# Hash attention and a gated feed-forward on one core: a new order of the first microseconds, one PSUM bank apart, and another issuer for the last pieces

## The chip, the core and the metric

The kernel runs on one core of a Trainium2 chip. The core has a matrix engine (TensorE, PE in the profile, with PEld for its weight loads), VectorE (DVE), ScalarE (ACT), GpSimd (POOL) and the sync engine (SP); SP, ACT and POOL can issue DMAs. The metric is device time in microseconds, the median of several runs.

## The reference, cut to what matters

```python
B, H, S, D = 4, 8, 768, 64            # attention; then 3072 tokens, 512 -> 2048 -> 512
q_bits = einsum(q, proj) > 0           # 6 bits; k_bits likewise
mask   = bucket(q_bits)[:, None] == bucket(k_bits)[None, :]
scores = where(mask, q @ k.T / 8, -1e9)
attn   = softmax(scores) @ v
x      = attn with heads side by side  # (3072, 512)
h      = x @ w_in
out    = (h * erf(softplus(h))) @ w_out
```

All inputs are float32.

## The kernel before, in words

**Attention.** The 32 heads are worked in 16 pairs; the heads of a pair sit on the partitions 0 to 63 and 64 to 127. For each pair TensorE hashes q and k with `proj`, ScalarE takes the signs, and signs and bucket weights become bfloat16 rows `qb` and `kb` whose product is zero where the buckets agree and hugely negative where they do not. A score tile `st` (128 keys, two heads of 384 queries) is the sum of two products, one of these bits and one of the float32 q and k. A pair has four groups of three such tiles: `score(n, c)` with n counting groups over all pairs and c from 0 to 2. ScalarE's `exponential` writes each tile to `e_all`, VectorE adds up the keys (`sum_keys`), and TensorE's `weigh` multiplies with v into `av` (L631). ScalarE's `leave` copies `av` out of PSUM (L690); the division by the sums follows later.

**Two ways for the bits.** Pair 0's bits are taken directly. `hash_bits` (L373) makes both halves of the rows with 64 output columns for q and 64 for k, one half of the 768 positions at a time; `take_bits` is ScalarE's sign (L386), two VectorE multiplies by the bucket weights (`spread_bits`, L397) and a VectorE copy (`double_bits`, L407), into the tile `both[0]`. All later pairs go another way: `bits_of` (L812) packs q and k of both halves into four groups of 32 columns, `sign_of` and `weigh_bits` work on the packed tile `sg`, `leave_bits` (L841) sends it to DRAM and `place_bits` (L850) brings it back into the right rows of `both[i % 2]`. The unused rows of `both` have to be zero: GpSimd clears `both[1]` at the start (L433), and `clean` (L859) clears `both[0]` after pair 0.

**PSUM.** Tiles of the tag `big` are two banks each, three of them: hashes and scores take them in turn, in the order in which they are allocated. `bank(...)` is one bank under one tag, and each call allocates it anew. `av` has one bank of the pool `psum`. In the feed-forward the pool `ps_f` holds seven banks, `M1` to `M7`.

**Order.** The start is written out by hand: loads, then `WARM` matmuls on a tile of ones (L780), then hashes and bits of pair 0. From there a planner, `arrange`, orders operations for each engine from estimated costs, ranks and due times; TensorE's own order is fixed by a list (`order`, `chain`), in which the first scores are followed by pair 1's bits, then `weigh`, and so on. VectorE and ScalarE also turn the weights into float32 between these operations, while GpSimd fetches the weights' pieces.

**Feed-forward.** Both matrix products use Strassen-like sums in blocks: seven products `P1` to `P7` (L1183) for the first, seven accumulations `M1` to `M7` (L1323) for the second, over six tiles of 512 tokens with four steps each. `combine` (L1354) adds the seven sums into output pieces and issues their DMA (L1362); `M3` is emptied last, in two halves k = 7 and k = 8. After that a flag decides on a general path, which these inputs do not need.

Of the kernel before, what the change touches and what calls it, by code (L numbers as in the profile page):

```python
# [54 lines left out]
F32 = mybir.dt.float32  # L55
# [8 lines left out]
P = 128  # L64
# [129 lines left out]
def kernel(  # L194
# [34 lines left out]
    small = ctx.enter_context(tc.tile_pool(name="small", bufs=3))  # L229
    QR = 32  # L230
    QB = QR // 2
    WARM = 5
    proj_sb = const.tile([P, 2 * QR], F32, name="proj_sb")
    weight = const.tile([P, 2], F32, name="weight")
    proj_q = const.tile([P, QR], F32, name="proj_q")
# [9 lines left out]
    blocks = []  # L245
    stats = const.tile([P, 2, NPAIR, 2], F32, name="stats")
    nc.vector.memset(ones, 1.0)
    nc.vector.memset(w_sum[:, 0, 0, 0:HS], 1.0)
    warm = w_sum[:, 0, 0, 0:HS]
    proj_in = const.tile([P, 2 * NBIT], F32, name="proj_in")  # L250
    nc.gpsimd.dma_start(out=proj_in, in_=proj2)
    nc.vector.memset(proj_sb, 0.0)
# [46 lines left out]
    def bank(name):  # L299
        return misc.tile([P, 512], F32, name=name, tag="bank")  # L300
# [108 lines left out]
    def take_bits(d, tile_of, halves=(0, 1)):  # L409
        cols = slice(halves[0] * HS, (halves[-1] + 1) * HS)  # L410
        sign_bits(d, tile_of, cols)
        for ab in (1, 0):
            spread_bits(d, cols, ab)
        double_bits(d, cols)

    def attention():
        NS = NPAIR * 4
        with (
# [4 lines left out]
            tc.tile_pool(name="rawp", bufs=2) as rawp,  # L423
            tc.tile_pool(name="cvt", bufs=1) as cvt,
            tc.tile_pool(name="psum", bufs=1, space=PSUM) as psum,
        ):

            def big(name):
# [1 line left out]

            sg = bitp.tile([P, HS], BF16, name="sg")
            both = [bitp.tile([P, 2, S], BF16, name=f"both{n}") for n in range(2)]
            nc.gpsimd.memset(both[1], 0.0)  # L433
            junk = ep.tile([P, HS], BF16, name="junk")
            NE = 3 * GC
            e_all = ep.tile([P, NE, 2, HS + 1], F32, name="e_all")
# [184 lines left out]
            def weigh(n):  # L621
                half, g = n // 2 % 2, n % 2
                d = pairs[n // 4]
                if g == 0:
                    d["av"] = psum.tile([P, 512], F32, name="av", tag="av")
                w = HS + 1 - half
                for c in range(GC):
                    e = block(n, c)
                    for ab in range(2):
                        rows = slice(ab * D, ab * D + D)  # L630
                        nc.tensor.matmul(  # L631
                            out=d["av"][rows, 0:w],
                            lhsT=d["v"][:, g * GC + c, rows],
                            rhs=e[:, ab, 0:w],
                            start=(g == 0 and c == 0),
                            stop=(g == 1 and c == GC - 1),
                        )
# [138 lines left out]
                pairs[i] = fetch(i, load)  # L776

            pairs[0] = fetch(0, load, quick=True)
            for n in range(WARM):
                nc.tensor.matmul(  # L780
                    out=bank("warm")[:, 0 : 2 * P],
                    lhsT=warm[:, 0:P],
                    rhs=warm[:, P:HS],
                    start=True,
                    stop=True,
                )
            for half in range(2):
                hash_bits(pairs[0], big, (half,))
                take_bits(pairs[0], lambda what: both[0][:, "qk".index(what[0]), :], (half,))

            NH = NPAIR * 2
            ops = []
# [5 lines left out]
            def pe(fn, args, cost, after=()):  # L798
                if chain:
                    after += (chain[-1],)  # L800
                op(fn, args, "PE", cost, (0, len(chain)), after, late=0.25)
                chain.append((fn.__name__,) + args)

            def bits_of(i):


                d = pairs[i]
                d["bits"] = big("bits")
                for n, what in enumerate("qk"):
                    for half in range(2):  # L810
                        row = (2 * n + half) * QR
                        nc.tensor.matmul(  # L812
                            out=d["bits"][row : row + QR, 0, 0:HS],
                            lhsT=proj_q,
                            rhs=d[what][:, half * HS : (half + 1) * HS],
                            start=True,
                            stop=True,
                        )
# [35 lines left out]
                        in_=bd[:, ab, 0 : NBIT + 1, :].rearrange("n r c -> r n c"),  # L854
                    )

            def clean():

                nc.gpsimd.memset(both[0], 0.0)  # L859

            chain = []
            order = [("score", 0)]
            for h in range(NH):
                order += [("score", n) for n in (2 * h + 1, 2 * h + 2) if n < NS]
                if h == 0:
                    order.insert(3, ("bits", 1))
                if h % 2 and (h + 3) // 2 < NPAIR:
                    order.append(("bits", (h + 3) // 2))
                if h >= 1:
                    order.append(("divisor", h - 1))  # L870
                order += [("weigh", 2 * h), ("weigh", 2 * h + 1)]
            slots = []
            for what, n in order:
                if what == "score":
                    i = n // 4
                    after = (("place_bits", i),)
                    if n == 0:
                        for c in range(2):
                            pe(plain, (n, c), 0.66)
                    for c in range(GC):  # L880
                        free = (slots[-3],) if len(slots) >= 3 else ()
                        pe(score, (n, c), 0.82 if n or c == 2 else 0.17, after + free)
                        slots.append(("exponential", n, c))
                elif what == "bits":
                    pe(bits_of, (n,), 0.92, (("start_pair", n), slots[-3]))
                    slots.append(("sign_of", n))
                elif what == "divisor":
                    pe(divisor, (n,), 0.42, (("sum_keys", n, last_sum(n)), ("keep_divisor", n - 1)))
                else:
                    h = n // 2  # L890
                    after = (("exponential", n, GC - 1),)
                    if n % 2 == 0:
                        after += (("leave", h - 1), ("leave_plain", (h - 1) // 2))
                    pe(weigh, (n,), 2.02, after)
# [42 lines left out]
            for i in range(NPAIR):  # L937
                n = 4 * i
                if i:
                    op(  # L940
                        start_pair,
                        (i,),
                        "SP",
                        3.6,
                        (0, n - 6),
                        (("weigh", n - 9), ("bits_of", i - 1))
                        + tuple(("measure", i - 3, m, half) for m in range(2) for half in range(2)),
                        late=3.5,
                    )
                    op(sign_of, (i,), "ACT", 0.6, (0, n - 6, 9), (("bits_of", i), ("leave_bits", i - 1)))  # L950
                    op(weigh_bits, (i,), "DVE", 0.33, (0, n - 6, 1), (("sign_of", i),))
                    op(leave_bits, (i,), "POOL", 0.7, (0, n - 6, 2), (("weigh_bits", i),), late=2.6)
                    op(
                        place_bits,
                        (i,),
                        "POOL",
                        1.2,
                        (0, n - 6, 3),
                        (("leave_bits", i), ("score", n - 5, 2)) + (("clean",),) * (i == 2),
                        late=2.6,  # L960
                    )
                for m in range(2):
                    for half in range(2):
                        op(
# [21 lines left out]
                )  # L986
                op(normalise, (i,), "DVE", 0.95, (0, n + 8, 4), (("widen", i), ("leave", 2 * i + 1)))
                op(send, (i,), "SP", 0.35, (0, n, 4), (("normalise", i),), late=2.2)
            op(clean, (), "POOL", 1.4, (0, 0), (("score", 3, 2),), late=0.3)
            for n in range(len(pieces)):  # L990
                op(
                    fetch_weights,
# [144 lines left out]
    def feed_forward(check, late):  # L1137
        again = late is None
        with (
# [3 lines left out]
            tc.tile_pool(name="work", bufs=1) as work,  # L1143
            tc.tile_pool(name="outp", bufs=1) as outp,
            tc.tile_pool(name="ps_f", bufs=1, space=PSUM) as ps_f,
        ):
            NTILE = NT // T
            NP = NTILE * NC4
# [6 lines left out]
            def product(p, name, where, first, last):  # L1155
# [19 lines left out]
                if first:  # L1175
                    if where == "X":
                        d[where] = bank("X")[:, :].rearrange("p (u t) -> p u t", u=2)
                    else:
                        d[where] = ps_f.tile([P, 2, TH], F32, name=where, tag=where)
                for u in range(2):  # L1180
                    f = (2 * c + u) * P
                    for kc in range(2):
# [123 lines left out]
            def project(p, name, k):  # L1306
# [11 lines left out]
                    M7=lambda: (d["h", 1][:, 0, :, :], w_block(c, 0, 1)),  # L1318
                )[name]()
                if c == 0 and k == 0:  # L1320
                    banks[name] = ps_f.tile([P, 2, TH], F32, name=name, tag=name)
                sub, u = divmod(k, 2)
                nc.tensor.matmul(  # L1323
                    out=banks[name][:, sub, :],
# [9 lines left out]
            def combine(t, k):  # L1334
# [24 lines left out]
                )  # L1359
                if where:  # L1360
                    r0 = t * T + where[0] * TH + subs.start * P
                    nc.sync.dma_start(  # L1362
                        out=out[
                            r0 : r0 + (subs.stop - subs.start) * P,
                            where[1] * TH : (where[1] + 1) * TH,
                        ].rearrange("(s p) d -> p s d", p=P),
                        in_=outs[into][:, subs, :],
                    )
# [395 lines left out]
```

## Time and profile before

| | |
|---|---|
| median of 10 runs | 919.16 us (918.52 to 920.0) |
| the profiled execution | 918.66 us, its span 916.8 us |
| PE, DVE, ACT, POOL busy | 99%, 89%, 84%, 5% |
| first hash on PE | 7.67 us |
| first complete score on PE | 12.30 us |
| pair 1's bits in place | 26.60 us |
| last av issued, first feed-forward product | up to 323.7, 324.23 us |
| last output DMA issued | 911.70 us |

A row of the profile's timeline gives start and duration in microseconds, engine, line of the kernel, operation, `out<-in`, shape and count, and in brackets how long the engine was idle before and which operation ended that. A row of the waits gives the waiting engine and line, then who released it, with the total, the number of times and the longest wait. The chain is the sequence of work that ended last, followed back from the last instruction.

### The profile page before, as it was taken

The numbers are of one execution on the slowest core, as the hardware profiler recorded it, in microseconds if no ns is written. First come the engines' busy times: TensorE is split into PE (matmuls) and PEld (weight loads), VectorE is DVE, ScalarE is ACT, GpSimd is POOL, SyncE is SP. The second block draws the span as 40 slices with busy tenths as digits, with TensorE's granted clock in tenths as the row PEclk, the third lists the DMA queues.
The fourth block names the chain that finished last, engine by engine and source line by source line (L and its number), as shares of the span: only waits on it lengthen the run. The fifth ranks groups of instructions, "written<-read, shape, count | busy, mean of one in ns | idle before, by whom it ended". The sixth has DMA issues, their size and how long they took to land.

```text
span 916.8 us, 13120 instructions
## 1 busy us (share of the span) xinstructions
PE 905.3 (99%) x5006; PEld 660.1 (72%) x5006; DVE 819.5 (89%) x1020; ACT 767.9 (84%) x1002; POOL 46.5 (5%) x83
## 2 busy tenths in 40 slices
PE   9999999999999999999999999999999999999997
PEld 4444444444444478888888888888888888888885
DVE  4899999999899979899999799988899889988995
ACT  5888887788887849999998998899989997899892
POOL 1211111111111000000000000000000000000000
PEclk9999999999999999999999999999999999999999
DMA  8455577655673131102022112211221121011201
GB/s 206 117 156 160 158 182 195 186 144 159 164 196 123 59 122 64 46 1 104 12 71 79 36 46 69 81 35 46 70 81 35 35 75 41 35 35 46 69 35 49
DMA packets 62966, 83.05 MB, mean 91 GB/s; under 512 B 34174, under 2 KB 47342, under 8 KB 62896
## 3 DMA queue, kind: packets, MB, share of 16 engines
q1 hardware_dynamic: 56672, 64.08, 24.3%
q0 software_dynamic: 6064, 17.86, 6.3%
q8 instruction: 41, 0.67, 0.3%
q14 instruction: 29, 0.24, 0.1%
q10 hardware_dynamic: 160, 0.20, 0.1%
HBM read 64.71 MB, written 17.40 MB: 90 GB/s over the span
## 4 chain that ended last, share of the span: by engine, by line
PE 95%; DVE 2%; DMA 1%; SPq 1%; ACT 0%; issue 0%; POOL 0%; DVEq 0%; ACTq 0%; POOLq 0%
PE M L1323 31%; PE X L1183 28%; PE st L550 16%; PE av L631 14%; PE M L1183 3%; PE z_ps L666 1%; PE bits L812 1%; DMA q<-in_qkT_dram 1%; SPq L358 1%; DVE e L1237 0%; DVE h L1265 0%; SPq L363 0%; DMA bd<-sg 0%; DMA both<-bd 0%; DVE S L1280 0%
## 5 line engine op out<-in xcount | busy, mean ns | idle before, releaser
L1250 DVE SCALAR_TENSOR_TENSOR e<-w,e 128x1024 f32<-128x1024 f32 x144 | 173.4, 1221 | 5.8 <-ACT w L1246 3.0
L568 ACT ACTIVATE e_all<-st 128x768 f32<-128x768 f32 x192 | 151.1, 812 | 14.0 <-PE st L550 12.6
L1246 ACT ACTIVATE w<-w,cq 128x1024 f32<-128x1024 f32 x144 | 160.6, 1143 | 1.9
L550 PE MATMUL st<-q,k 64*128 64x384 f32 x768 | 155.7, 484 | 0.0
L1323 PE MATMUL M<-w_out_sb,h 128*128 128x256 f32 x576 | 140.3, 380 | 0.4 <-DVE h L1265 0.4
L631 PE MATMUL av<-e_all,v 128*64 128x385 f32 (+1 forms) x768 | 131.2, 490 | 0.0
L1183 PE MATMUL X<-x,w_in_sb 128*128 128x256 f32 x512 | 121.2, 380 | 0.0
L1323 PEld LDWEIGHTS M<-w_out_sb,h 128*128 128x128 f32 x576 | 109.4, 190 | 15.7 <-DVE h L1265 1.1
L1183 PEld LDWEIGHTS X<-x,w_in_sb 128*128 128x128 f32 x512 | 97.2, 190 | 13.7 <-ACT h L1201 0.6
L631 PEld LDWEIGHTS av<-e_all,v 128*64 128x64 f32 x768 | 52.3, 136 | 67.5 <-issue 66.6
L550 PEld LDWEIGHTS st<-q,k 64*128 64x128 f32 x768 | 68.7, 189 | 35.4 <-issue 34.5
L1323 PE MATMUL M<-wt,S 128*128 128x256 f32 x384 | 93.5, 380 | 0.4 <-DVE S L1280 0.4
L1183 PE MATMUL X<-x_sum,w_sum 128*128 128x256 f32 x344 | 81.7, 381 | 1.8 <-ACT h L1201 1.8
L1323 PEld LDWEIGHTS M<-wt,S 128*128 128x128 f32 x384 | 73.0, 190 | 10.6 <-DVE S L1280 0.8
L1183 PEld LDWEIGHTS X<-x_sum,w_sum 128*128 128x128 f32 x344 | 65.1, 190 | 11.9 <-ACT h L1201 3.3
L1201 ACT COPY h<-X 128x512 f32<-128x512 f32 x85 | 49.0, 576 | 22.3 <-PE X L1183 21.4
L1227 DVE SCALAR_TENSOR_TENSOR w<-w,e 128x1024 f32<-128x1024 f32 x48 | 58.5, 1221 | 9.7 <-ACT w L1222 9.6
L550 PE MATMUL st<-both 64*128 64x384 bf16 x384 | 63.2, 324 | 0.4 <-DMA both<-bd 0.2
L1265 DVE TENSOR_TENSOR h<-h,e 128x1024 f32<-128x1024 f32 x48 | 58.0, 1221 | 5.8 <-ACT e L1261 5.5
L1241 ACT ACTIVATE w<-e 128x1024 f32<-128x1024 f32 x48 | 50.4, 1050 | 13.3 <-DVE e L1237 13.0
L1237 DVE TENSOR_TENSOR e<-e,w 128x1024 f32<-128x1024 f32 x48 | 57.5, 1218 | 2.7 <-ACT e L1233 2.6
L1205 DVE TENSOR_TENSOR h<-X,h 128x512 f32<-128x512 f32 x65 | 44.8, 690 | 16.3 <-PE X L1183 15.4
(133 smaller groups left out, 1378.0 us busy)
## 6 DMA issues: line engine op xcount, KB each, us to landing
wt<-wt SPq DMA_DIRECT2D x24, 768.0 KB, 4.1
raw<-in_w_out_dram POOLq DMA_DIRECT2D x16, 512.0 KB, 4.6
raw<-in_w_in_dram POOLq DMA_DIRECT2D x14, 512.0 KB, 4.3
v<-in_v_dram SPq DMA_DIRECT2D x32, 192.0 KB, 4.6
xs<-x SPq DMA_DIRECT2D x16, 384.0 KB, 2.7
q<-in_qkT_dram SPq DMA_DIRECT2D x30, 192.0 KB, 4.1
k<-in_qkT_dram SPq DMA_DIRECT2D x30, 192.0 KB, 4.3
r<-rd SPq DMA_DIRECT2D x30, 192.0 KB, 3.4
```

The costliest lines, as they stand in the source:

```text
L550: nc.tensor.matmul(out=st[:, ab, 0:HS], lhsT=d["k" + src][rows, keys], rhs=d["q" + src][rows, cols], start=(part == 0), stop=(part == 1),)
L568: nc.scalar.activation(out=e[:, :, 0:HS], in_=st[:, :, 0:HS], func=AF.Exp, scale=scale)
L631: nc.tensor.matmul(out=d["av"][rows, 0:w], lhsT=d["v"][:, g * GC + c, rows], rhs=e[:, ab, 0:w], start=(g == 0 and c == 0), stop=(g == 1 an ...
L1183: nc.tensor.matmul(out=d[where][:, u, :], lhsT=a[:, kc, f : f + P], rhs=b[:, kc, :], start=(first and u == 0 and kc == 0), stop=(last and ...
L1201: nc.scalar.copy(out=quarter(p, q), in_=st[p][where])
L1227: nc.vector.scalar_tensor_tensor(out=w, in0=w, scalar=-1.0, in1=st[p]["e", v], op0=ALU.add, op1=ALU.subtract)
L1237: nc.vector.tensor_tensor(out=s, in0=s, in1=st[p].pop(("w", v)), op=ALU.subtract)
L1241: nc.scalar.activation(out=z, in_=st[p]["s", v], func=AF.Square)
L1246: nc.scalar.activation(out=q, in_=z, func=AF.Square, bias=cq[:, j : j + 1])
L1250: nc.vector.scalar_tensor_tensor(out=s, in0=st[p].pop(("q", v, j)), scalar=ERF_Q[j][1], in1=s, op0=ALU.add, op1=ALU.mult,)
L1265: nc.vector.tensor_tensor(out=h, in0=h, in1=st[p].pop(("s", v)), op=ALU.mult)
L1323: nc.tensor.matmul(out=banks[name][:, sub, :], lhsT=a[:, u, sub * P : (sub + 1) * P], rhs=b[:, u, :], start=(c == 0 and k == 0), stop=(c = ...
```

## The change

The start: twice as many warm-up matmuls with half as many columns, on the constant `ones` in place of a tile filled for it, into a PSUM tile taken once; the two plain (float32) parts of the first scores are put between the hashes of the two halves. Pair 1's bits are made as pair 0's, in `both[1]`, without the way through DRAM; `both[1]` is cleared after pair 1 in place of at the start. The planner is told of later due times for `leave_bits` and `place_bits` of the other pairs. `av` gets a pool and so a bank of its own, which in the feed-forward is that of `M3`. The last two output pieces are issued by ScalarE's queue.

```diff
-    WARM = 5
+    WARM = 10
...
-    nc.vector.memset(w_sum[:, 0, 0, 0:HS], 1.0)
-    warm = w_sum[:, 0, 0, 0:HS]
...
+            tc.tile_pool(name="psum_v", bufs=1, space=PSUM) as psum_v,
...
-            nc.gpsimd.memset(both[1], 0.0)
...
-                    d["av"] = psum.tile([P, 512], F32, name="av", tag="av")
+                    d["av"] = psum_v.tile([P, 512], F32, name="av", tag="av")
...
+            warm = bank("warm")
             for n in range(WARM):
                 nc.tensor.matmul(
-                    out=bank("warm")[:, 0 : 2 * P],
-                    lhsT=warm[:, 0:P],
-                    rhs=warm[:, P:HS],
+                    out=warm[0:D, 0:P],
+                    lhsT=ones,
+                    rhs=ones[:, 0:1].broadcast_to([P, P]),
...
             for half in range(2):
                 hash_bits(pairs[0], big, (half,))
                 take_bits(pairs[0], lambda what: both[0][:, "qk".index(what[0]), :], (half,))
+                if half == 0:
+                    for c in range(2):
+                        plain(0, c)
...
             def bits_of(i):
+                if i == 1:
+                    hash_bits(pairs[i], big)
+                    return
...
-            def clean():
-                nc.gpsimd.memset(both[0], 0.0)
+            def place_first():
+                cols = slice(0, S)
+                sign_bits(pairs[1], lambda what: both[1][:, "qk".index(what[0]), :], cols)
+            def weigh_first(ab):
+                spread_bits(pairs[1], slice(0, S), ab)
+            def double_first():
+                double_bits(pairs[1], slice(0, S))
+            def clean(n):
+                nc.gpsimd.memset(both[n], 0.0)
...
                 if h == 0:
-                    order.insert(3, ("bits", 1))
+                    order.append(("bits", 1))
...
-                    after = (("place_bits", i),)
-                    if n == 0:
-                        for c in range(2):
-                            pe(plain, (n, c), 0.66)
+                    after = (("double_first",) if i == 1 else ("place_bits", i),)
...
+                    if i == 1:
+                        op(place_first, (), "ACT", 0.9, (0, n - 2, 9), (("bits_of", i),))
+                        for ab in (1, 0):
+                            op(weigh_first, (ab,), "DVE", 0.43, (0, n - 2, 1), (("place_first",),))
+                        op(double_first, (), "DVE", 0.35, (0, n - 2, 2), (("weigh_first", 0), ("weigh_first", 1)))
+                    else:
...
-                    op(leave_bits, (i,), "POOL", 0.7, (0, n - 6, 2), (("weigh_bits", i),), late=2.6)
+                        op(leave_bits, (i,), "POOL", 0.7, (0, n - 6, 2), (("weigh_bits", i),), late=3.6)
...
-            op(clean, (), "POOL", 1.4, (0, 0), (("score", 3, 2),), late=0.3)
+            for n in range(2):
+                op(clean, (n,), "POOL", 1.4, (0, 4 * n), (("score", 4 * n + 3, 2),), late=0.3)
...
+            tc.tile_pool(name="ps_l", bufs=1, space=PSUM) as ps_l,
...
-                        d[where] = ps_f.tile([P, 2, TH], F32, name=where, tag=where)
+                        d[where] = (ps_l if where == "M3" else ps_f).tile([P, 2, TH], F32, name=where, tag=where)
...
-                    banks[name] = ps_f.tile([P, 2, TH], F32, name=name, tag=name)
+                    banks[name] = (ps_l if name == "M3" else ps_f).tile([P, 2, TH], F32, name=name, tag=name)
...
-                    nc.sync.dma_start(
+                    queue = nc.scalar if k >= 7 and t == NTILE - 1 else nc.sync
+                    queue.dma_start(
```

More of the change, by code (lines that the diff above doesn't have):

```diff
@@ L884, in attention @@
                 elif what == "bits":
-                    pe(bits_of, (n,), 0.92, (("start_pair", n), slots[-3]))
-                    slots.append(("sign_of", n))
+                    pe(bits_of, (n,), 0.92 if n > 1 else 1.44, (("start_pair", n), slots[-3]))
+                    slots.append(("sign_of", n) if n > 1 else ("place_first",))
                 elif what == "divisor":
@@ L949, in attention @@
                     )
-                    op(sign_of, (i,), "ACT", 0.6, (0, n - 6, 9), (("bits_of", i), ("leave_bits", i - 1)))
-                    op(weigh_bits, (i,), "DVE", 0.33, (0, n - 6, 1), (("sign_of", i),))
-                    op(leave_bits, (i,), "POOL", 0.7, (0, n - 6, 2), (("weigh_bits", i),), late=2.6)
[L953 to L961, printed above, removed]
+                    if i == 1:
[4 more added lines that the diff above has]
+                    else:
+                        op(sign_of, (i,), "ACT", 0.6, (0, n - 6, 9), (("bits_of", i), ("leave_bits", i - 1)))
+                        op(weigh_bits, (i,), "DVE", 0.33, (0, n - 6, 1), (("sign_of", i),))
+                        op(leave_bits, (i,), "POOL", 0.7, (0, n - 6, 2), (("weigh_bits", i),), late=3.6)
+                        op(
+                            place_bits,
+                            (i,),
+                            "POOL",
+                            1.2,
+                            (0, n - 6, 3),
+                            (("leave_bits", i), ("score", n - 5, 2), ("clean", i - 2)),
+                            late=3.6,
+                        )
                 for m in range(2):
```

## The prediction

> **What bounds the kernel now.** I read the page's engine shares and chain first, then the first 30 us in order of time, the waits around the change of stage at 324 us, and the last 10 us.
>
> ```profile
> PE 905.3 (99%) x5006; PEld 660.1 (72%) x5006; DVE 819.5 (89%) x1020; ACT 767.9 (84%) x1002; POOL 46.5 (5%) x83
> ...
> PE 95%; DVE 2%; DMA 1%; SPq 1%; ACT 0%; issue 0%; POOL 0%; DVEq 0%; ACTq 0%; POOLq 0%
> ```
>
> TensorE (PE) is busy for 99% and carries 95% of the chain that ended last. The table by stretches has PE at 20.00 of every 20 us from 40 to 320 us, and the list of PE's waits between 30 and 320 us is empty. So what moves PE's start or closes one of its holes moves the end by as much. The holes are where the change works:
>
> ```profile
> 0.82 0.11 DVE L247 MEMSET ones<- 128x64 f32 x1 [0.82 <-PEq L1744]
> ...
> 1.40 6.34 PE L780 MATMUL warm<-w_sum 128*128 128x256 f32 x10 [1.40 <-DVE w_sum L248]
> ...
> 2.67 0.50 PEld L780 LDWEIGHTS warm<-w_sum 128*128 128x128 f32 x2 [0.78 <-PE warm L780]
> ...
> 4.14 0.34 DVE L255 COPY proj_sb<-proj_in 64x6 f32<-64x6 f32 x2 [2.61 <-DMA proj_in<-in_proj_dram]
> ...
> 8.36 0.85 PE L373 MATMUL bits<-q,proj_sb 128*64 128x384 f32 x1
> ...
> 9.00 0.85 PE L373 MATMUL bits<-q,proj_sb 128*64 128x384 f32 x1
> ...
> 10.43 2.04 PE L550 MATMUL st<-q,k 64*128 64x384 f32 x8
> ...
> 10.59 0.25 DVE L407 COPY both<-both 64x384 bf16<-64x384 bf16 x1
> ...
> 12.30 0.65 PE L550 MATMUL st<-both 64*128 64x384 bf16 x6
> ...
> 12.69 5.92 ACT L568 ACTIVATE e_all<-st 128x768 f32<-128x768 f32 x8 [1.54 <-PE st L550]
> ...
> 18.50 0.52 PE L812 MATMUL bits<-q,proj_q 128*32 128x384 f32 x2
> ...
> 19.29 4.10 PE L631 MATMUL av<-e_all,v 128*64 128x385 f32 x24
> ```
>
> (Start, duration, engine, line; ten warm records are five calls.) The warm block ends at 7.7 and only then the hashes (L373) begin. Each warm call takes 1.28 us: its weight load waits 0.78 us for the call before. The hash records follow each other at 0.64 us, score records of the same 384 columns later at 0.32: until about 11.4 us TensorE runs at half clock, though the page's clock row shows 9 there. The first complete score starts at 12.30. The next hole, as the chain of waits has it:
>
> ```profile
> 20.94 2.19 DMA bd<-sg
> ...
> 23.15 0.02 POOLq L850
> ...
> 23.81 0.57 POOL both L850
> 24.38 2.17 DMA both<-bd
> ...
> 26.60 2.59 PE st L550 x17
> ```
>
> Pair 1's bits travel through DRAM, and PE gets them at 26.60. Then the change of stage (waiting engine, releaser, us in total):
>
> ```profile
> PEld M L1183 <- ACT x L690: 1.2, 1, 1.2
> ...
> PE M L1183 <- ACT x L690: 0.6, 1, 0.6
> ```
>
> The first feed-forward product waits for ScalarE (ACT) to copy the last av out of PSUM. And the tail:
>
> ```profile
> 910.42 0.76 DVE L1354 TENSOR_TENSOR u<-M,u 128x256 f32<-128x256 f32 x2 [0.44 <-PE M L1323]
> 910.87 0.83 SPq L1362 DMA_DIRECT2D out_dram<-u  x2
> ```
>
> SP issues the last two pieces until 911.70; 5.1 us later the span ends.
>
> **What the skill says.** "TensorE: Matmul & The Clock Gate", Part 1: the array starts at half clock and is released after one busy window of about 3.4 us; windows run free of the kernel's start. The trace agrees: dense records from 7.67, doubling near 11.4, 3.8 us later; the gapped warm block of 6.3 us released nothing. "DMA: Bandwidth & Descriptors", Issuing engines are not separate DMA queues: another issuing engine saves only issue time. Here ACT's two first k issues took 1.21 us, SP's like-sized pairs 1.19 to 1.47: no cheaper. "PSUM — Partial Sum Buffer", Specifications: eight banks. The kernel uses all: one bank, three double ones, one for av; the new pool adds none.
>
> **The change part by part.**
>
> *1. Warm block.* Ones are ready at 0.93 instead of w_sum at 1.34, so it starts near 0.98. Ten calls of two records, 128 columns each: at half clock 0.64/3 = 0.21 us of streaming, beside a 64-column weight load (0.23 in the hash rows). If loads overlap streams as in the hashes, 20 x 0.23 = 4.6, ending at **5.6**; between 4.9 (clock released early) and 9.8 (load and stream in turn, 0.44). I take 5.6, because the tile is now taken once, so no call should wait for the one before. First-half q and k cover it: last issue at 1.40, median landing 3.1 us, so 4.5 (with the longest, 4.4 us, 5.8); proj_sb is ready at 4.48.
>
> *2. Order hash, two plain scores, hash.* Work is 0.64 + 1.28 + 0.64 = 2.56 us at full clock, twice that at half. Release: 4.8 if the half-width warm calls count (0.98 + 3.8), 9.4 if not (5.6 + 3.8); I choose 7.0. Then hash to 6.9, plain scores to 8.2, second hash to **8.9**. Its q has landed (issued at 4.18, plus 3.1 = 7.3). The masked part needs the first half's signs and bits: that took from 8.95 to 10.84, 1.9 us, so ready at 8.8; it no longer has the second hash alone as cover and is what is late next: no start before 5.6 + 0.64 + 1.9 = 8.1. With release at 9.4 the start is 10.1 (with none, 5.6 + 5.12 = 10.7). Gain against 12.30: **3.4** (2.2 to 4.2).
>
> *3. PSUM ring.* Taking the double banks in order, both plain scores are now allocated ahead of the second hash. The third score then needs the bank of the first, so waits for the first exponential. That ended at 13.5, 1.26 us after 12.30; before, the third score started 0.34 after. Queued behind it: every later score, and the exponentials fed by them. From complete first score to pair 1's bits: now 18.50 - 12.30 = 6.20; then 1.26 + 7 x 0.81 = 6.93. **Loss 0.73.**
>
> *4. Pair 1's bits.* L812 took 0.79 (18.50 to 19.29); hash_bits with two 64-column outputs takes 4 x 0.32 = 1.28. **Loss 0.49.** Its k, issued by 7.92 and landing in 4.1 us, is there at 12.0, needed at 15.8. ACT's sign grows from 0.58 to about 0.9, DVE gets two multiplies and a copy (about 1.6 us for 0.33): hidden under the 4.03 us of av and 2.43 us of score 3 that PE does meanwhile. With that, the bits are ready some 3 us ahead of score 4; PE now idles from 25.75 to 26.60. **Gain 0.85.** Two DRAM transfers and three POOL issues (1.7 us) vanish, off the path.
>
> *5. POOL memsets.* One of 1.40 us leaves the start, where nobody waits, and returns as a second clean ahead of pair 3's place_bits. POOL is 5% busy, and behind a clean stand place_bits and weight fetches; PE never waited for place_bits after pair 1. The changed due time (late 3.6) can reorder ACT and DVE later; PE's empty wait list is the cover: 0. If the cover were gone, each late landing would cost PE its delay.
>
> *6. Change of stage.* av in its own bank, later M3's: the first product no longer waits for the copy. av's next matmul elsewhere starts just before its modelled end (19.29 + 4.10 against 23.32), so product 1 can start near 323.6 instead of 324.23. **Gain 0.6** (0.5 to 0.7; 0 if another wait stands there).
>
> *7. Tail.* ACT issues the two u pieces; by DVE's ends (10.84 and 11.18 past 900) no earlier than SP, as SP's piece before ended at 910.38. But SP is free 1.3 us sooner for its exit, while ACT's exit starts later and both wait for the landing. The 5.1 us aren't itemised, so I bound it: loss 0.3 to gain 0.8. I take **0.4**.
>
> Sum: 3.4 - 0.73 - 0.49 + 0.85 + 0.6 + 0.4 = **4.0 us**. The profiled execution took 918.66 (span 916.8 and 1.9 around), 0.50 below the median of 919.16: it would take 914.6, the median **915.1**. Nothing later absorbs the gain: PE is busy in 100.00 of 100 us in three of the feed-forward's stretches.
>
> **Rivals.** What measurement can tell from no change is about 0.2%, 1.8 us.
>
> *Only the front works* (0.12). A further wait stands before product 1, and the tail is set by the landing: 919.16 - 3.0 = 916.1. For it: no view itemises the 5.1 us of the tail. Against, at the product: ACT is the only releaser named.
>
> *The warm calls still wait for each other* (0.10), as rewrites of one place. The 0.78 us waits speak for it; that the tile was then taken anew each time speaks against. Each call then costs 0.43 streaming plus today's 1.28 - 0.85 = 0.43: 8.6, ending at 9.6. Hash to 10.9, plain scores (release at 11.4) to 12.4, second hash 13.0: 0.7 late in place of 3.4 early, total -0.1: **919.2**, no change.
>
> *The clock stays at half* (0.06), the slower one. At T = 10.7, all at half clock, the sum is 1.6 - 0.73 - 0.49 + 0.85 + 1.0 = 2.2; each further us at half costs 0.5. Even at 15.1, slower by 0.2% from 18.8; release at 22 gives 919.16 - 2.2 + 5.65 = **922.6**. For it: 6.3 us of gapped warm-up released nothing, the new calls fill half the columns, and part 3 puts a 0.9 us hole behind them. Against: 3.8 dense microseconds were enough, and PE is dense from 0.98 on.
>
> **How the numbers follow.** My forecast has 0.69 with its own range 913.8 (4.2 - 0.73 - 0.49 + 0.85 + 0.7 + 0.8 = 5.3) to 917.1 (2.2, 0.5 and -0.3 in place of 3.4, 0.6 and 0.4: 2.0); front alone 0.12; no change 0.10; clock 0.06; 0.03 for a reorder that costs PE elsewhere. Faster: 0.81, within: 0.10, slower: 0.09. The range takes 913.5 to 918.2: the forecast, the front alone, a part of the waiting warm-up.
>
> **What would show it.** Warm records without the 0.78 us waits, ending near 5.6; first score on bits near 8.9 and first exponential near 9.3; a PE hole of 0.9 us before the third score; pair 1's bits near 15.8 and no DRAM transfer for them; score 4 without a wait near 23.5; no ACT releaser at the first L1183 product; a span near 912.8. Wrong if hashes start after 8, if score records stay 0.64 apart beyond 11, or if PE's waits between 30 and 320 us aren't empty.

## The result, and the profile after

The changed kernel takes 915.32 us (914.62 to 916.27), the kernel before, run beside it, 919.43: a ratio of 0.9955 with a 95% interval of 0.9945 to 0.9964, or 4.1 us. The profiled execution took 915.49 us with a span of 913.7; its span is 3.1 us shorter than the one shown of before. The sum forecast 4.0 us, and the median 915.1.

The steps of the sum against the two profiled executions (microseconds; gains are positive):

| step | forecast | trace | read from |
|---|---|---|---|
| 1 and 2: first complete score | 3.4 | 3.84 | 12.30, now 8.46 |
| 3: third score waits for a bank | -0.73 | -0.33 | first complete score to pair 1's bits: 6.20, now 6.53 |
| 4: longer bit product | -0.49 | -0.55 | 0.79, now 1.34 |
| 4: no hole ahead of score 4 | 0.85 | 0.69 | see below |
| 5: POOL's queue and due times | 0 | -1.26 | lead lost near 63 us (1.17) and 237 us (0.09) |
| 6: change of stage | 0.6 | 0.65 | first product 324.23, now 321.20: 3.03, less the lead of 2.38 before it |
| 7: tail | 0.4 | 0.08 | last DVE piece to the end: 6.03, now 5.95 |
| sum | 4.0 | 3.12 | spans: 3.1 |

The front first, rows of the timeline of the changed kernel (start, duration, engine, line, operation, in brackets the idle time before and what ended it):

```profile
0.99 4.53 PE L779 MATMUL warm<-ones 128*64 128x128 f32 x20 [0.99 <-DVE ones L247]
...
8.46 0.50 PE L548 MATMUL st<-both 64*128 64x384 bf16 x4
...
9.23 0.34 PE L548 MATMUL st<-both 64*128 64x384 bf16 x2 [0.28 <-ACT both L384]
...
14.99 0.54 PE L371 MATMUL bits<-q,proj_sb 128*64 128x384 f32 x1
...
16.33 4.05 PE L629 MATMUL av<-e_all,v 128*64 128x385 f32 x24
...
22.75 0.33 PE L548 MATMUL st<-both 64*128 64x384 bf16 x2
```

Twenty warm records in 4.53 us, without a wait between them. The third score waits, but for the sign of the second half (L384), and only from 8.95 to 9.23. Pair 1's bits are hashed directly at 14.99, and score 4 starts at 22.75 with no wait in front. The hole that is gone was smaller than the 0.85 us of the forecast, as one row of the kernel before shows:

```profile
26.03 0.32 PE L550 MATMUL st<-both 64*128 64x384 bf16 x1
```

One of score 4's two bit products ran there inside the stretch that the forecast counted as idle; only the second waited until 26.60. PE's lead over the kernel before is 2.96 us at the first av (19.29, now 16.33) and 3.64 at the next (30.23, now 26.59), so the hole was worth 0.69.

At the change of stage, two rows of the timeline:

```profile
317.18 4.09 PE L629 MATMUL av<-e_all,v 128*64 128x384 f32 x24
321.20 1.13 PE L1204 MATMUL M<-x,w_in_sb 128*128 128x256 f32 x4
```

The first product stands directly behind the last av, and ACT is no releaser any more. But earlier, in the attention stage, a wait has appeared where the list of before was empty. The waits of PE between 20 and 318 us (waiting engine, releaser; total, times, longest):

```profile
PE st L548 <- ACT e_all L566: 1.1, 1, 1.1
```

and the timeline around it:

```profile
48.62 0.55 POOL L846 DMA_DIRECT2D bd<-sg  x1 [5.17 <-DVE sg L836]
...
55.32 1.15 POOL L855 DMA_DIRECT2D both<-bd  x2 [6.15 <-issue]
...
56.46 1.14 POOL L454 DMA_DIRECT2D raw<-in_w_in_dram  x2
...
60.72 0.68 ACT L468 ACTIVATE keep<-raw 128x512 f32<-128x512 f32 x1 [4.49 <-DMA raw<-in_w_in_dram]
...
63.28 0.34 PE L548 MATMUL st<-both 64*128 64x384 bf16 x2 [1.10 <-ACT e_all L566]
```

Read from the bottom: PE waits 1.10 us for an exponential. ACT is late with it because `square_high` (L468) stands ahead of it in ACT's fixed order and waited 4.49 us for a weight piece. That piece was issued by POOL at 56.46, because `place_bits` of pair 3 stands ahead of it in POOL's queue, and POOL stood idle for 6.15 us in front of that. The row names no releaser ("issue"); but pair 3's bits, sent to DRAM at 48.62, landed at 54.69, and this landing is what `place_bits` has to wait for. Two rows of the kernel before:

```profile
52.02 0.55 POOL L841 DMA_DIRECT2D bd<-sg  x1 [7.96 <-DVE sg L831]
...
63.18 0.68 ACT L470 ACTIVATE keep<-raw 128x512 f32<-128x512 f32 x1 [3.31 <-DMA raw<-in_w_in_dram]
```

ACT waited for the weight piece there too, but PE did not feel it. The bits now leave 3.40 us earlier, nearly as much as PE's lead of 3.64; but their transfer took 6.07 us in place of 4.06, so that `place_bits`, the fetch and `square_high` come only 1.4, 1.4 and 2.5 us earlier (before at 56.71, 57.84 and 63.18).

The tail, one line of the waits of SP in the last 10 us:

```profile
SPq L1730 <- SPq L1730: 3.9, 4, 3.1
```

and one of the timeline:

```profile
907.87 1.79 ACTq L1384 DMA_DIRECT2D out_dram<-u  x2
```

SP's branch over the general path takes 3.1 us (2.8 before) and now begins before the last pieces are issued, but three further waits follow it (0.8 us together, on the semaphores of the last pieces), where before there were none; ACT takes 1.79 us to issue what SP issued in 0.83, and at the very end SP waits another 0.4 us for ACT's own branch.

### The profile page after: what moved, and what is told of

It is laid out like the page before. It is cut to its first block, busy times and chain, and to the rows that moved or that the text cites. A ratio compares the mean times of both kernels' runs of the same rounds, so it can differ in the third digit from the quotient of the medians.

```text
span 913.7 us, 13136 instructions
## 1 busy us (share of the span) xinstructions
PE 902.4 (99%) x5016; PEld 661.1 (72%) x5016; DVE 819.6 (90%) x1021; ACT 767.7 (84%) x1002; POOL 45.1 (5%) x80
## 4 chain that ended last, share of the span: by engine, by line
PE 91%; DVE 2%; issue 1%; DMA 1%; ACT 0%; POOL 0%; DVEq 0%; ACTq 0%; POOLq 0%
PE M L1344 31%; PE X L1204 28%; PE st L548 14%; PE av L629 12%; PE M L1204 3%; PE z_ps L664 1%; PE bits L817 1%; DMA raw<-in_w_in_dram 0%; DVE e L1258 0%; DVE h L1286 0%; DVE S L1301 0%; DVE h L1226 0%; DVE x_sum L340 0%; DVE w L1248 0%; ACT h L1222 0%
```

## The experiments

All were timed in five rounds beside the kernel before; four kernels at a time shared a chip.

**Does the wait near 63 us come back?** The changed kernel, nothing edited, twice.

> The changed kernel, nothing edited: a second profiled execution, to see whether PE's one wait of the middle comes back (1.10 us at 63.28 us, behind a bit transfer of pair 3 that took 6.1 us from issue to landing where before it took 4.1). Theory one, a transfer that happened to be late in that execution: PE's waits between 30 and 320 us are empty, and the span is near 913.7 - 1.1 = 912.6. Theory two, the new order of the program makes it: the wait is there again at 62 to 64 us, between 0.8 and 1.4 us, and the span is within 0.3 of 913.7. The median by itself is 915.3 in both.

> The changed kernel once more, beside the kernel with the earlier fetch on the same chip. The wait near 63 us was 1.10 and 0.30 us in its two profiles so far; if it is a race between PE and a chain of transfers it is there again with another length between 0.2 and 1.2. Median 915.0 to 915.4.

It came back in both: 0.30 us in a span of 913.4, and 0.8 us in a span of 913.0. The medians are 915.06 (914.31 to 915.82) and 915.27 (914.82 to 915.41). So neither theory of the first text stands as written: the order of the program makes the wait, and how late the transfers are in an execution sets its length.

**Where the wait is made.** One dependence in the planner's list moves one POOL instruction; no other engine's order changes. It was run twice, the second time beside the changed kernel.

```diff
-                            (("leave_bits", i), ("score", n - 5, 2), ("clean", i - 2)),
+                            (("leave_bits", i), ("score", n - 5, 2), ("clean", i - 2)) + (("fetch_weights", 5),) * (i == 3),
```

> The changed kernel with one POOL instruction moved: the fetch of weight piece 5 stands ahead of place_bits of pair 3, not behind it. All other engines keep their order. Theory one, PE's wait near 63 us is the end of a chain (bits of pair 3 land, place_bits, weight fetch, ACT's square_high that stands ahead of the exponential): the piece now lands 3 us or more sooner, PE's waits between 30 and 320 us are empty, PE keeps its 3.7 us lead over the kernel before up to 320 us, and the time is 0.3 to 1.1 us shorter. Rival, the exponential would have come late anyway (ACT is behind for its own work, or the bits of pair 3 are what it needs): the wait stays within 0.3 us of what it was, no gain.

> The kernel with the fetch of weight piece 5 ahead of place_bits, once more beside the changed kernel on the same chip. Theory one: no wait near 63 us, and the median 0.5 to 0.9 us below the changed kernel's. Rival: the 0.7 us between the two medians so far came from the chip or from where the clock was released, and here they are within 0.3 of each other.

The timeline of POOL in the first of them:

```profile
49.18 0.53 POOL L454 DMA_DIRECT2D raw<-in_w_in_dram  x1 [0.17 <-issue]
54.41 1.15 POOL L855 DMA_DIRECT2D both<-bd  x2 [4.70 <-DMA bd<-sg]
```

The weight piece now leaves at 49.18 in place of 56.46, and `place_bits` still waits 4.70 us for its bits, with nothing late behind it. PE waits nowhere from 10.3 to 330 us in either profile, and the lead over the kernel before is kept: 3.78 us at 55 us and 3.88 at 316. Medians 914.37 and 914.45; beside the changed kernel's 915.27 that is 0.8 us less, with runs (914.08 to 914.88 against 914.82 to 915.41) that hardly touch. Theory one holds in both texts: the chain through POOL's queue makes the wait. The bits of pair 3 were not what PE needed, and the second clean, which this kernel keeps, was not the cause.

**The warm-up, its length.** `WARM = 10` to `WARM = 5`.

> The changed kernel with 5 warm calls in place of 10: 2.3 us less of warm-up, ending near 3.2. The first hash can't start before its q and signs, 5.28 in the changed kernel. Theory one, the warm block's unbroken length is what releases the clock: PE idles from 3.2 to 5.3, the hashes and plain scores run with records 0.64 apart for some 3.5 us more, the first score on bits starts between 10 and 10.7 in place of 8.46, and the time is 1.3 to 2.3 us longer. Theory two, the window only counts a share of busy time: release near 5 to 7 still, first score on bits 8.5 to 9.2, time 0 to 0.7 longer. Theory three, the landing alone sets the start: no difference.

```profile
5.16 0.87 PE L371 MATMUL bits<-q,proj_sb 128*64 128x384 f32 x1 [1.78 <-DMA q<-in_qkT_dram]
...
6.74 2.62 PE L548 MATMUL st<-q,k 64*128 64x384 f32 x8
...
10.08 0.50 PE L548 MATMUL st<-both 64*128 64x384 bf16 x4
```

The hashes can't start sooner, since q lands then; PE idles 1.78 us ahead of them, and hashes and plain scores run at half clock (2.62 us for eight records that take 1.56 in the changed kernel). The first complete score comes at 10.08, and the median is 917.04, 2.0 us above the changed kernel on the same chip, as theory one says. (The profiled execution, 915.72, was one of the faster ones: the runs lie between 914.91 and 917.94.) The extra five calls bring no result, but they keep PE dense until q is there.

**The warm-up, its tile.** The tile is taken anew for each call: `out=bank("warm")[0:D, 0:P]`.

> The changed kernel with the warm tile taken anew for each of the ten calls, as the kernel before did for its five. Theory one, the prediction's first step: taking it anew is what makes a call wait for the one before; each call then costs some 0.86 us, the block ends near 9.6, the hashes start there, and the time is 3 to 4.5 us longer than the changed kernel's. Rival: the waits of the kernel before came from its 128-column weights loaded into a busy array, not from the tile, and the block ends near 5.2 as before: no difference.

The waits of PE's weight loads in the first 12 us:

```profile
PEld warm L778 <- PE warm L778: 4.1, 9, 0.5
```

Nine of ten calls wait 0.45 us for the call before; each costs 0.74 us, the hashes begin at 7.96, the records turn short only near 12, and the first complete score comes at 13.18. The median is 919.6: 4.3 us above the changed kernel, and level with the kernel before (1.0003, 0.9995 to 1.0011). So without this one detail the whole gain is gone: ten dense calls in 4.5 us bring the clock that ten waiting ones in 7 us don't.

**The order of the first scores.** One plain score behind each half of the hash.

```diff
-                if half == 0:
-                    for c in range(2):
-                        plain(0, c)
+                plain(0, half)
```

> The changed kernel with one plain score behind each half of the hash (hash, plain, hash, plain) in place of both behind the first. Theory one: the second hash is done 0.66 us sooner, so the second half's sign on ACT no longer stands ahead of the first exponential and the third score's bank is free when PE gets there: the hole of 0.43 us before the third score closes, the first score on bits starts at 8.3 to 8.5 as before, and the time is 0.3 to 0.5 us shorter. Rival: the signs and bits of the first half then come 0.65 us too late for PE (they take 1.9 us from the end of the first hash, and only one plain score and one hash, 1.4 us, cover them), the first score on bits is unchanged or later, and the gain is 0 or a loss of up to 0.5.

```profile
8.60 0.65 PE L548 MATMUL st<-both 64*128 64x384 bf16 x6
...
9.86 0.34 PE L548 MATMUL st<-both 64*128 64x384 bf16 x2
```

The hole before the third score closed (six records in one run from 8.60), as theory one says, but the first score came 0.14 us later than in the profile shown above and the fourth comes 0.13 us late (9.09 to 9.86, in the changed kernel 9.40 to 10.04), so a little of the rival holds too. From the first hash to pair 1's bits it is 9.66 us, in the repeated changed kernel 9.71; the medians are 915.14 and 915.06. No gain. What took it: the second hash has to wait until 6.97 for the second half of q, which landed at 6.83. With two plain scores ahead of it that landing is covered. The mixed order with the earlier fetch, and the same with SP's tail:

> The order hash, plain, hash, plain and the earlier fetch of weight piece 5 together. If the fetch removes the wait: PE's lead over the kernel before stays at 3.8 us from 26 to 320 us, the change of stage adds 0.6, the span is near 912.2 and the median 914.0 to 914.4, 0.7 to 1.1 us below the changed kernel. If not: as the mixed order alone, 915.1.

> The kernel with mixed order and earlier fetch, with all output pieces on SP. The tail in six profiles, from the start of the last DVE sum to the end of the span: SP 6.03 and 6.21 us, ACT 5.95, 6.64, 5.94 and 5.80, so theory one says ACT's issues are worth nothing that shows: within 0.3 us of the same kernel with ACT's issues. Rival one, the 1.1 us between the medians of the first such pair was the tail: 0.8 to 1.4 us slower. Rival two, the prediction's term: 0.4 us slower.

The first took 914.23 us (913.71 to 914.54), span 912.4 and no wait from 8 to 330 us: the gain is the fetch's, and the mixed order can't be told from the other. The second is spoken of next.

**The tail.** The last pieces by SP, in two bases: `queue = nc.sync`.

> The changed kernel with all output pieces issued by SP again. Theory one: ACT's issues are worth the 0.1 us that the two spans show from the last DVE piece to the end (6.38 before, 6.28 after), so the median is 0 to 0.2 above the changed kernel's, and the last piece lands as before. The prediction's term: 0.4 us slower than the changed kernel. Rival: ACT's second issue, 1.39 us long in place of 0.40, costs more than it saves, and this kernel is 0.2 to 0.5 us faster.

Medians: 916.16 against 915.06, and 914.79 against 914.23. SP's version is 1.1 and 0.6 us slower in the pairs, yet the intervals of their ratios to the kernel before overlap (0.9936 to 0.997 against 0.9926 to 0.996 in the first), and the profiles show little of it in the tail. From the start of the last DVE sum to the end, ACT's ten profiles lie between 5.80 and 6.64 us (mean 6.14), SP's four are 6.01, 6.03, 6.21 and 7.10. The second of two issues took either 0.4 to 0.5 or 1.4 to 1.9 us, on SP as on ACT. In both SP profiles of the changed front the clock was released late, at 6 to 7 us, which a tail can't bring about. What is left: an estimate of 0 to 0.3 us for the tail from these profiles (the means differ by 0.2); whether the larger difference of the medians is more than the chance of the clock's release stays open.

**The way of pair 1's bits.** The changed kernel with the fourth step undone and, since the second clean and the later due times go with it, the fifth too; the front, the bank and the tail are kept.

```diff
+            nc.gpsimd.memset(both[1], 0.0)
...
-                if i == 1:
-                    hash_bits(pairs[i], big)
-                    return
...
-                    order.append(("bits", 1))
+                    order.insert(3, ("bits", 1))
...
-                    if i == 1:
-                        op(place_first, (), "ACT", 0.9, (0, n - 2, 9), (("bits_of", i),))
...
-            for n in range(2):
+            for n in range(1):
                 op(clean, (n,), "POOL", 1.4, (0, 4 * n), (("score", 4 * n + 3, 2),), late=0.3)
```

> The changed kernel with pair 1's bits as before: hashed with 32-column outputs, sent through DRAM by POOL, both[1] cleared at the start. Theory one, the prediction's fourth step: the bit product takes 0.79 in place of 1.34 us, the way from its end to score 4 takes the 7.3 us of the kernel before and PE idles 0.85 us, so score 4 starts 0.3 us later than in the changed kernel; the wait near 63 us takes up to that back, and the time is 0 to 0.4 us longer. Rival, the transfers of pair 1's bits now fall together with the loads of pairs 1 and 2 and take longer: a hole of 1.5 to 3 us and a time 1 to 2 us longer.

```profile
19.02 0.55 POOL L844 DMA_DIRECT2D bd<-sg  x1 [15.17 <-DVE sg L834]
...
24.29 1.14 POOL L853 DMA_DIRECT2D both<-bd  x2 [4.72 <-DMA bd<-sg]
...
28.61 0.61 PE L549 MATMUL st<-both 64*128 64x384 bf16 x2 [5.75 <-DMA both<-bd]
...
28.88 1.62 PE L549 MATMUL st<-q,k 64*128 64x384 f32 x4
```

The DMA issues of that stretch, with KB each and median time to landing:

```profile
bd<-sg POOLq DMA_DIRECT2D x1, 96.0 KB, 4.6
both<-bd POOLq DMA_DIRECT2D x2, 21.0 KB, 4.0
```

The median is 921.97 us: 6.9 us above the changed kernel's 915.06 of another chip, and slower than the kernel before (1.0022, 1.0009 to 1.0035). Both theories fall short, though the rival named the mechanism: the two transfers take 4.6 and 4.0 us (before 2.2 and 2.1). The first leaves while the DMA engines are still over 80% busy with the start's loads (until about 22 us), the second meets the q and k loads that SP issues at 22.95 and 24.16; in the kernel before both fell into a quieter stretch. PE idles 5.75 us. Then comes what neither text had: after this hole PE runs at half clock (1.62 us for four records that take 0.81), with a granted clock of 0.64 from 28 to 36 us. "TensorE: Matmul & The Clock Gate" of the Trainium skill, Part 1, states this: after an idle window of about 3.4 us the clock falls back to half. The trace agrees. At the second half-pair's av this profile is 8.2 us behind the changed one: some 5.9 by the hole (score 4 at 28.61 in place of 22.75) and 2.3 by the clock (6.16 us from there to the av in place of 3.84). It was the slowest of the runs (923.70).

**The bank alone**, in the kernel before: `psum_v` for `av`, `ps_l` for `M3`.

> The kernel before with one part of the change: av, and later the third feed-forward sum M3, in a PSUM bank of their own. Theory one, the prediction's sixth step: ACT is no longer a releaser of the first feed-forward product, which starts directly behind the last av, 0.58 to 0.6 us sooner (323.6 in place of 324.23), nothing else moves, and the time is 0.6 us shorter than the kernel before. Rival: banks are handed out anew, and another product or the first score of a half-pair waits for a bank, so that the span gains less than 0.3 or loses.

```profile
320.02 4.09 PE L632 MATMUL av<-e_all,v 128*64 128x384 f32 x24
324.04 1.13 PE L1185 MATMUL M<-x,w_in_sb 128*128 128x256 f32 x4
```

No wait stands between the two rows. From the first issue of the last av to the first product it is 4.02 us, in the kernel before 4.67: 0.65 gained, as theory one says. The median, 918.58 against 919.65, goes the same way, but the ratio (0.9995, 0.9985 to 1.0006) doesn't resolve it, and the profile shows other differences as large. Its front is that of the kernel before, and yet the clock was released near 10.0 in place of 11.4 us and the first complete score came at 11.63, 0.67 us sooner; nearly all of that was lost again ahead of score 4, where pair 1's bits still had to come through DRAM (its second bit product at 26.51, before 26.60), and near 63 us PE waited 0.5 us.

## Why the prediction was right, point by point

*Steps 1 and 2, the front.* Right in mechanism. The hashes begin at 5.28, 0.3 us before where step 1 put them, because the tile is taken once; the kernel that takes it anew gave 919.6 where that rival was priced at 919.2. The release at 7.0 was a choice between 4.8 and 9.4, and no reason was given for the middle. In ten profiles with ten warm calls and the tile taken once, the records turn short between 3.9 and 6.8 us, in four of them before the first hash; so the half-width calls do count. The first complete score lies between 8.07 and 9.11; the forecast's 8.9 is near the late end. The kernel before has such a spread too (12.30 here, 11.63 in the profile with the bank alone), so the 3.84 of the table is the difference of two single executions. The windows that run free of the kernel's start ("TensorE: Matmul & The Clock Gate" of the Trainium skill, Part 1) would account for the spread, but no run here shows them. The window of about 3.4 us that the page gives fits the kernel with five calls (release near 8.9, 3.7 us after the hashes begin); the earliest release seen, 2.9 us after the first warm record, is below it, and there the measurement stands.

*Step 3, the bank.* The direction was right and the term mis-sized: 0.33 in place of 0.73. "Taking the double banks in order" failed. The third score got the bank of the second hash, which is free as soon as its sign is done at 9.18; the first exponential ended at 9.89. The mixed order shows the same: there the sign is early, the third score doesn't wait, and the fourth does.

*Step 4, pair 1's bits.* The mechanism was right. The longer product cost 0.55 (forecast 0.49); the hole was worth 0.69 in place of 0.85, because "PE now idles from 25.75 to 26.60" misread the rows: one of score 4's bit products ran at 26.03. What the sum didn't say is that the front can't stand without this step: with the new front and the DRAM way, the kernel is 8.2 us behind by the second half-pair. No run has the direct way with the old front.

*Step 5, POOL.* This is the step that failed. It named the right queue ("behind a clean stand place_bits and weight fetches") and then took PE's empty wait list as cover at 0. The wait is 0.2 to 1.1 us in seven of eight profiles that have the changed kernel's place of that fetch (the kernel with five warm calls has none), and absent with the fetch moved, in four of four. The cover was thin in any case: PE waits 0.5 us there in the profile with the bank alone, with no more than 0.1 us of lead over the kernel before, 0.2 with the warm tile taken anew (1.1 us behind it), and 0.55 with pair 1's bits through DRAM (4.5 us behind it). The four longest waits (0.8 to 1.1) fall on leads of 3.0 to 4.0 us, but a lead of 3.8 met only 0.3, and the five calls' 2.0 none: that the lead lengthens the wait is likely, but not shown apart from how long the transfers take. The second clean and the changed due times aren't needed for it: the kernel with the DRAM way has neither and waits.

*Step 6.* 0.65 here and 0.65 alone; forecast 0.6.

*Step 7, the tail.* Mis-sized: 0.08 in place of 0.4. SP's exit did become free sooner, but its branch now ends before the landings, and these and ACT's own exit take its place, a case that the lower bound held. "Runtime: NRT & Kernel Launch" of the Trainium skill, Instruction fetch mechanics, states that a taken branch out of the current window has to fetch its target by DMA. In the fourteen profiles the branch takes 2.7 to 3.1 us on SP and 2.4 to 2.8 on ACT; no run shows that a fetch is what fills them.

Taken together, the front (0.4) and the third score's bank (0.4) were better than forecast, POOL's part, the tail and the hole ahead of score 4 (1.26, 0.3 and 0.2) worse: the traces show 3.1 us in place of 4.0. The medians show 4.1, since the profiled execution of before lay 0.5 us or more under its median and that of after 0.2 over. So that the forecast of 915.1 meets 915.3 so closely is in part luck: errors of opposite sign, and the choice of executions. The wait of step 5 is real: without it the kernel takes 914.4.

## What to carry to other kernels

An empty list of waits says nothing of how near the next wait is: before a gain of some microseconds early in a kernel is booked to its end, follow the chains that feed the bottleneck (DMA landings, an in-order queue with an issue behind a waiting one, an engine's fixed order) and ask of every link whether it comes earlier by as much. Here the first link did, by 3.4 us, and the landing behind it by 1.4. In an in-order DMA queue, put the transfer that is ready ahead of the one that waits; here one such exchange was worth 0.8 us. And a lead that outruns a transfer can cost more than the lead: the hole of 5.75 us also took the clock.

## What was not expected of the hardware

- The same ten warm calls had the clock released between 3.9 and 6.8 us in ten executions, and the first complete score came between 8.07 and 9.11; with the front of before it was 12.30 and 11.63.
- A hole of 5.75 us was followed by some 5 us at half clock, 2.3 us more; the hole of at most 0.85 us in the kernel before has no such trace.
- The same 96 KB transfer to DRAM took 2.2 us to land when the start's loads were running out (DMA share 0.73, then 0.15) and 4.6 under them (1.17, then 1.04). Pair 3's took 4.1 us in one kernel and 4.9 to 6.1 in three executions of another; what lengthens it was not looked into.
- The second of two back-to-back DMA issues took 0.4 to 0.5 us in some executions and 1.4 to 1.9 in others, on SP and on ACT.
